# One level of Strassen's scheme in the first product of layer 2, over pairs of feature tiles and 768-token superblocks

## The chip, the cores and the metric

The kernel runs on one core of a Trainium2 chip, in one launch. The metric is the device time of the execution in microseconds (us). Three executions of the kernel before took 1248.97, 1250.37 and 1250.49 us (median 1250.37). One execution was profiled; all durations below come from it.

## The reference

A chunked attention with eight memory keys per head feeds two feed-forward layers of 3072 tokens, 512 model and 2048 hidden features. All is computed to float32 accuracy.

```python
# attention: per chunk of 32 queries, keys from 16 before to 8 after, plus 8 memory keys
x = attn_out.transpose(0, 2, 1, 3).reshape(B * S, H * D)      # 3072 x 512
h = x @ w_in;  sp = log1p(exp(h));  x = (h * tanh(sp)) @ w_out            # layer 1
h = x @ w2_in; g = h * (1 / (1 + exp(-1.702 * h))); out = g @ w2_out      # layer 2
```

## The kernel before, in words

Tokens are cut into 8 blocks of 384 (`TB`), hidden features into 16 tiles of 128 (`NF`), model features into 4 tiles of 128 (`KD`). Every float32 operand of a product is split into two fp32r parts, a high one and the rest (`xh`, `xl`; `wi` and `wo` hold both parts side by side; `gh`, `gl`), and a product is three matmuls: high by high, low by high, high by low.

A step of layer 1 or 2 is one block j and one feature tile f. Its first product (`gemm1`, L792) has 4 x 3 matmuls of 384 columns that fill one PSUM bank `h` (there are two). In layer 2 ScalarE then computes a tanh (L806), VectorE multiplies by h (L808), rounds to `gh` (L815) and subtracts to get `gl` (L821). The second product (`gemm2`, L840) adds into banks `o`: in layer 2 three token tiles, 3 matmuls of 512 columns each. After 16 steps the three banks are evacuated (L858 on ScalarE or L861 on VectorE) into the buffers `e` and `ev`, two of each, and written out.

Layer 1 works while attention for the next block runs beside it. Its result goes to DRAM (`x1d`) and is fetched for layer 2 through staging tiles `st` (a ring of two buffers). The weights arrive as 64-bit words and are converted to float32; those of layer 2 are converted during layer 1, kept in DRAM (`w2d`), and fetched and split once near the end of layer 1 (`w2_fetch`), after which they stay in SBUF.

The order on every engine is set by a planner in the kernel (class `Plan`): each operation has a rank and a guessed duration per engine, an operation goes to an engine when its inputs are ready and its rank is lowest, and the resulting order is then written out, fixed. The guesses are formulas such as `dve(n) = (65 + 1.052 n) / 1000` us for a VectorE operation of n columns. On the chip each engine works through its list in that order, and a wait of the first instruction holds all behind it. All loads and stores around the change are issued by SyncE's queue (SP), in order too.

Of the kernel before, what the change touches and what calls it, by code (L numbers as in the profile page):

```python
# [238 lines left out]
def kernel(  # L239
# [29 lines left out]
    L1 = NB * NF  # L269
    NQ = H // 2 * (GB // 2)  # L270
# [507 lines left out]
    xin = {}  # L778
    outs = {}

    def step(layer, j, f):
        i = ((layer - 1) * NB + j) * NF + f
        xh, xl = x0[j] if layer == 1 else xin[j]
        wh, wl = wi[layer, f]
# [15 lines left out]
        if layer == 1:  # L800

            add(i + 0.3, [("act", act(TB, True), lambda: nc.scalar.activation(  # L802
                out=u.get(), in_=h.get(), func=AF.Mish))], reads=[h], writes=[u], table="mish")
        else:

            add(i + 0.3, [("act", act(TB, True), lambda: nc.scalar.activation(  # L806
                out=u.get(), in_=h.get(), func=AF.Tanh, scale=0.851))], reads=[h], writes=[u], table="exp")
            add(i + 0.6, [("dve", dve(TB), lambda: stt(  # L808
                out=u.get(), in0=u.get(), scalar=1.0, in1=h.get(), op0=ALU.add, op1=ALU.mult
            ))], reads=[h], updates=[u])  # L810
        gh, gl = (T[n].new([P, TB], F32R) for n in ("gh", "gl"))
        add(
            i + 0.65,
# [7 lines left out]
        add(i + 0.7, [("dve", dve(TB), lambda: nc.vector.tensor_tensor(  # L821
            out=gl.get(), in0=u.get(), in1=gh.get(), op=ALU.subtract))], reads=[u, gh], writes=[gl])

        vh, vl = wo[layer, f]
        first, last = f == 0, f == NF - 1
        width = TB if layer == 1 else DM
        if first:
            outs[layer, j] = [
                (T[f"o{m}"].new([P, width], F32), []) for m in range(KD if layer == 1 else TB // P)
            ]  # L830
        for m, (o, order) in enumerate(outs[layer, j]):
            c = slice(m * P, (m + 1) * P)

            def gemm2(o=o, c=c):
                if layer == 1:
                    prods = ((vh[:, c], gh.get()), (vl[:, c], gh.get()), (vh[:, c], gl.get()))
                else:
                    prods = ((gh[:, c], vh.get()), (gh[:, c], vl.get()), (gl[:, c], vh.get()))
                for n, (a, b) in enumerate(prods):
                    nc.tensor.matmul(  # L840
                        out=o.get(), lhsT=a, rhs=b, start=(first and n == 0), stop=(last and n == 2)
                    )

            add(
                i + 2.3, [("pe", 3 * (width / 2400 + 0.003), gemm2)],
                reads=[vh, vl, gh, gl], writes=[o], chain=order,
            )

    def finish(layer, j):
        rank = ((layer - 1) * NB + j + 1) * NF + 1.4  # L850
        c = 1.0 if layer == 1 else 0.5
        width = TB if layer == 1 else DM
        x1s[j] = fixed()
        for m, (o, order) in enumerate(outs.pop((layer, j))):
            t = T["ev" if layer == 1 or m % 2 else "e"].new([P, width], F32)

            def by_act(o=o, t=t):
                nc.scalar.activation(out=t.get(), in_=o.get(), func=AF.Copy, scale=c)  # L858

            def by_dve(o=o, t=t):  # L860
                nc.vector.tensor_scalar(out=t.get(), in0=o.get(), scalar1=c, scalar2=None, op0=ALU.mult)  # L861

            ways = [("act", act(width, True), by_act), ("dve", dve(width), by_dve)]
            add(rank, ways if m % 2 == 0 else ways[::-1], reads=[o], writes=[t])
            if layer == 1:
                load(rank, x1s[j], [lambda t=t, m=m: (x1d[:, m, j * TB:(j + 1) * TB], t.get())],
                     P * TB * 4, 1536, [t])
            else:
                r0 = j * TB + m * P
                load(rank, x1s[j], [lambda t=t, r0=r0: (out[r0:r0 + P, :], t.get())], P * DM * 4, 2048, [t])  # L870
# [55 lines left out]
    for f in range(NF):  # L926
        w2_fetch(f, L1 - NF + f + 3)
    for j in range(NB):
        if j:
            x1_fetch(j)  # L930
        for f in range(NF):
            step(2, j, f)
# [33 lines left out]
```

## Time and profile before

| | us |
|---|---|
| median of three executions | 1250.37 |
| the profiled execution | 1246.88 |
| its span, first to last instruction | 1245.1 |
| TensorE busy | 1212.2 |
| VectorE busy | 724.9 |
| ScalarE busy | 484.9 |

In the profile a line is one group of instructions with the same code line, engine and operation; PE is TensorE, PEld its weight loads, DVE is VectorE, ACT is ScalarE, SP is the queue that issues DMAs. Matmuls overlap one another in the records, so that a matmul's own time (340 ns) is longer than its share of a full stretch; what one costs is read from the time between the starts of groups.

### The profile page before, as it was taken

To read this page: it belongs to the slowest core of one execution; us is meant where nothing else is said; L and a number is where in the kernel's file an instruction comes from. 1 tells how busy PE (TensorE), PEld (TensorE's weight loads), DVE (VectorE), ACT (ScalarE), POOL (GpSimd) and SP (SyncE) were. 2 spreads that over 40 slices of the span, in tenths; PEclk is the share of its full clock that TensorE was granted. 3 is DMA by queue.
4 is the path that set the end of the run, shared out by engine and by line. 5 is a ranking of instruction groups with operands and counts; after the bars stand their busy time and mean duration, and the time that the engine had idled before them with its cause. 6 is when DMAs were issued, how large, how long until landed. Compare 5 with 4: busy or idle time off the path is not lost.

```text
span 1245.1 us, 18734 instructions
## 1 busy us (share of the span) xinstructions
PE 1212.2 (97%) x6912; PEld 1126.8 (91%) x6912; DVE 724.9 (58%) x2074; ACT 484.9 (39%) x1091; POOL 8.2 (1%) x24
## 2 busy tenths in 40 slices
PE   7788899999999999999999999999999999999998
PEld 6687799999999999999999989999999999999997
DVE  6999976767777767677645534343433434343333
ACT  5777665555555555555434411111111111111111
POOL 1000000000000000000000000000000000000000
PEclk9899999999999999999999999999999999999999
DMA  9952343433333334343134401010010101000000
GB/s 214 256 176 107 79 116 74 115 88 92 97 90 99 97 86 106 81 95 90 52 120 134 148 13 44 9 26 26 1 52 1 51 1 51 1 26 1 26 1 26
DMA packets 167450, 92.36 MB, mean 74 GB/s; under 512 B 129272, under 2 KB 153863, under 8 KB 167359
## 3 DMA queue, kind: packets, MB, share of 16 engines
q1 hardware_dynamic: 167007, 90.42, 27.0%
q0 software_dynamic: 352, 0.75, 0.3%
q8 instruction: 54, 0.88, 0.3%
q14 instruction: 37, 0.30, 0.1%
HBM read 70.17 MB, written 20.97 MB: 73 GB/s over the span
## 4 chain that ended last, share of the span: by engine, by line
PE 90%; DVE 4%; SPq 2%; DMA 2%; ACT 1%; issue 1%; DVEq 0%; ACTq 0%
PE h L792 42%; PE o L840 41%; PE s L704 3%; SPq L297 2%; PE s L604 2%; PE s L678 1%; DMA vt<-in_v_dram 1%; DMA wi<-in_moe_w_in_dram 1%; DVE st L353 1%; DVE st L357 0%; DMA wi<-in_q_dram 0%; DVE wi L381 0%; DVE wo L381 0%; DMA vt<-in_mem_v_dram 0%; DVE gl L821 0%
## 5 line engine op out<-in xcount | busy, mean ns | idle before, releaser
L792 PE MATMUL h<-xh,wi 128*128 128x384 f32 x2048 | 534.4, 342 | 8.7 <-DVE wi L376 3.4
L792 PEld LDWEIGHTS h<-xh,wi 128*128 128x128 f32 x2048 | 373.3, 190 | 29.4 <-DVE wi L381 4.7
L792 PE MATMUL h<-xl,wi 128*128 128x384 f32 x1024 | 346.8, 339 | 0.0
L840 PE MATMUL o<-gh,wo 128*128 128x384 f32 x1024 | 274.9, 350 | 0.0
L840 PE MATMUL o<-wo,gh 128*128 128x512 f32 x768 | 240.1, 394 | 0.0
L808 DVE SCALAR_TENSOR_TENSOR u<-u,h 128x384 f32<-128x384 f32 x128 | 71.0, 555 | 288.9 <-ACT u L806 288.1
L806 ACT ACTIVATE u<-h 128x384 f32<-128x384 f32 x128 | 62.9, 492 | 437.1 <-PE h L792 437.1
L792 PEld LDWEIGHTS h<-xl,wi 128*128 128x128 f32 x1024 | 194.1, 190 | 0.0
L840 PEld LDWEIGHTS o<-gh,wo 128*128 128x128 f32 x1024 | 181.9, 189 | 1.3 <-issue 0.3
L840 PE MATMUL o<-gl,wo 128*128 128x384 f32 x512 | 172.7, 337 | 0.0
L840 PEld LDWEIGHTS o<-wo,gh 128*128 128x128 f32 x768 | 142.7, 188 | 23.2
L821 DVE TENSOR_TENSOR gl<-u,gh 128x384 fp32r<-128x384 f32 x256 | 142.4, 557 | 17.8 <-PE o L840 0.5
L840 PE MATMUL o<-wo,gl 128*128 128x512 f32 x384 | 151.9, 396 | 0.0
L802 ACT ACTIVATE u<-h 128x384 f32<-128x384 f32 x128 | 62.8, 491 | 135.2 <-PE h L792 119.1
L632 ACT ACTIVATE e<-e,mx 96x128 f32<-96x128 f32 x240 | 94.4, 395 | 51.0 <-DVE mx L617 50.8
L815 DVE CAST gh<-u 128x384 fp32r<-128x384 f32 x232 | 83.2, 359 | 36.6 <-ACT u L802 22.8
L840 PEld LDWEIGHTS o<-gl,wo 128*128 128x128 f32 x512 | 96.5, 189 | 0.0
L840 PEld LDWEIGHTS o<-wo,gl 128*128 128x128 f32 x384 | 72.1, 188 | 16.6
L617 DVE CUSTOM_DVE_ANT_0 e<-s,mask 96x128 f32<-96x128 f32 x240 | 56.0, 283 | 41.9 <-PE s L604 40.6
L802 ACT ACT_TABLE_LOAD x55 | 70.6, 1283 | 10.2 <-PE h L792 8.7
L632 ACT ACT_TABLE_LOAD x54 | 69.3, 1283 | 3.4 <-DVE mx L617 2.5
L685 DVE COPY aT<-s 128x384 f32<-128x384 f32 x49 | 27.3, 557 | 43.1 <-PE s L678 42.0
(104 smaller groups left out, 861.2 us busy)
## 6 DMA issues: line engine op xcount, KB each, us to landing
wi<-in_moe_w_in_dram SPq DMA_DIRECT2D x16, 512.0 KB
wo<-in_moe_w_out_dram SPq DMA_DIRECT2D x16, 512.0 KB
st<-in_moe_w_in_dram SPq DMA_DIRECT2D x16, 512.0 KB
st<-in_moe_w_out_dram SPq DMA_DIRECT2D x16, 512.0 KB
w2d<-v SPq DMA_DIRECT2D x32, 256.0 KB
st<-w2d SPq DMA_DIRECT2D x16, 512.0 KB
x1d<-ev SPq DMA_DIRECT2D x32, 192.0 KB
st<-x1d SPq DMA_DIRECT2D x16, 384.0 KB
```

The source lines that it names most:

```text
L297: queue.dma_start(out=o, in_=i)
L617: nc.vector.tensor_tensor_reduce(out=e[:, i, hh, :], in0=s[hh][:, i, :], in1=mask[:GQ, mask_of(g0 + i), :], scale=-scale, scalar=-NEG, op0 ...
L632: nc.scalar.activation(out=e[:, i, hh, :], in_=e[:, i, hh, :], func=AF.Exp, scale=-1.0, bias=mx[:, i, hh:hh + 1], accum_out=sm[:, i, hh:hh ...
L685: ("dve", dve(TB), lambda: nc.vector.tensor_copy(out=aT.get(), in_=t.get())),
L704: nc.tensor.matmul(out=o[:, i].rearrange("p h t -> p (h t)"), lhsT=vt[:, g + i, h:h + 2].rearrange("p h d -> p (h d)"), rhs=aT[:, i].rearr ...
L792: nc.tensor.matmul(out=h.get(), lhsT=a[:, c], rhs=b[:, kk, :], start=(n == 0), stop=(n == 3 * KD - 1))
L802: add(i + 0.3, [("act", act(TB, True), lambda: nc.scalar.activation(out=u.get(), in_=h.get(), func=AF.Mish))], reads=[h], writes=[u], tabl ...
L806: add(i + 0.3, [("act", act(TB, True), lambda: nc.scalar.activation(out=u.get(), in_=h.get(), func=AF.Tanh, scale=0.851))], reads=[h], wri ...
L808: add(i + 0.6, [("dve", dve(TB), lambda: stt(out=u.get(), in0=u.get(), scalar=1.0, in1=h.get(), op0=ALU.add, op1=ALU.mult))], reads=[h], u ...
L815: ("dve", dve(TB, True), lambda: nc.vector.tensor_copy(out=gh.get(), in_=u.get())),
L821: add(i + 0.7, [("dve", dve(TB), lambda: nc.vector.tensor_tensor(out=gl.get(), in0=u.get(), in1=gh.get(), op=ALU.subtract))], reads=[u, gh ...
L840: nc.tensor.matmul(out=o.get(), lhsT=a, rhs=b, start=(first and n == 0), stop=(last and n == 2))
```

## The change

Layer 1 is left as it was. In layer 2 two blocks of 384 tokens form a superblock (4 of them), and the feature tiles f and f + 8 form a pair (8 pairs; 32 pairs in all). The model features are cut into two halves of 256. So the first product of a pair is a 2 x 2 product of blocks (feature tile by half of the model features, times half of the model features by token block), and it is done with seven block products in place of eight, by Winograd's form of Strassen's scheme. Each block product is 2 x 3 matmuls of 384 columns.

The seven left operands are sums and differences of the weights' four blocks (`w2_pair`: four combinations of 256 columns, then high and low parts). In superblock 0 they are computed for each pair in turn from `w2d`, used, and stored to DRAM (`w2c`, `w2o`); superblocks 1 to 3 load them again from there, pair by pair. The seven right operands are combinations of the two token blocks (`x_prep`: per superblock four pieces of 192 columns; per piece two or three subtractions, and for each of its operands a high and a low part). They lie in twelve places, the buffers of `xh`, `xl` and of the first halves of `wi` and `wo`; operands 0 to 4 and 5 to 6 of the next superblock are made at different times.

In `step2` products 0 and 1 fill the two `h` banks, are read (`copy`, `plus`), and products 2 and 3 add to the same banks; the same follows with 4, 5 and 6. Five VectorE additions (`plus`, L1109) and two copies (L1103, ScalarE) per pair form the four blocks of h; each then goes through the same tanh, multiply, round and subtract as before (`gate`). The second products (`second`, L1065; 4 x 3 x 3 matmuls of 512 columns per pair) are those of the pair before, and stand between the first products. They add into six banks (`o0` to `o3`, `s0`, `s1`), which are evacuated into `ev` alone (two buffers).

```diff
+    w2c = dram.tile([NP, 4, P, 2 * DM], F32, name="w2c")
+    w2o = dram.tile([NF, P, 2 * DM], F32, name="w2o")
+    AT = ((0, 0), (1, 1), (0, 1), (2, 0), (1, 0), (3, 0), (2, 1))
...
+    def keep_split(rank, both, n, src, view):
...
+                ("act", act(n), lambda: nc.scalar.activation(out=hi.get(), in_=view(), func=AF.Copy)),
+                ("dve", dve(n, True), lambda: nc.vector.tensor_copy(out=hi.get(), in_=view())),
...
+        add(rank + 0.02, [("dve", dve(n), lambda: nc.vector.tensor_tensor(
+            out=lo.get(), in0=view(), in1=hi.get(), op=ALU.subtract))], reads=[*src, hi], writes=[lo])
...
+    def w2_pair(q):
+        sblk, p = divmod(q, NP)
+        base = L1 + 4 * q
+        A = [T[f"wi{NF // 2 + 4 * (p % 2) + i}"].new([P, 2 * DM], F32R) for i in range(4)]
+        O = [T[f"wo{NF // 2 + 2 * (p % 4) + i}"].new([P, 2 * DM], F32R) for i in range(2)]
+        if sblk:
...
+                    load(base - 3.5 + 0.1 * i, A[i], [lambda i=i: (A[i].get().bitcast(F32), w2c[p, i])],
+                         P * 8 * DM, 4096, [w2cs[p, i]])
...
+            return
...
+            st = T["st"].new([P, 2 * DM], F32)
+            load(base - 6 + 0.1 * i, st, [lambda st=st, f=f: (st.get(), w2d[f])], P * 8 * DM, 4096, [w2s[f]])
...
+        deps = [keep_split(base, A[0], DM, [a], lambda: a[:, 0:DM])]
+        s1 = comb(base + 0.1, 0, a21, a22, ALU.add, [b])
+        s2 = comb(base + 0.2, 1, lambda: x[:, 0], a11, ALU.subtract, [a, s1])
+        deps.append(keep_split(base + 0.4, A[1], DM, [s1, s2], lambda: x[:, 0:2].rearrange("p a c -> p (a c)")))
+        s3 = comb(base + 1.0, 2, a11, a21, ALU.subtract, [a, b])
+        s4 = comb(base + 1.1, 3, a12, lambda: x[:, 1], ALU.subtract, [a, s2])
...
+                load(base + 3, w2cs[p, i], [lambda i=i: (w2c[p, i], A[i].get().bitcast(F32))], P * 8 * DM, 4096, deps[i])
...
+    places = ["xh", "xl", "wi0", "wi2", "wi4", "wo0", "wo2", "xh", "xl", "wi6", "wo4", "wo6"]
...
+    def x_prep(sblk, wanted, pieces, rank, gap=0.0):
...
+            st = T["st"].new([P, 2, 2, HALF], F32)
...
+                t1 = comb(rank, 2, lambda st=st, w=w: sub(
+                    out=w[:, 0:2], in0=st[:, :, 1], in1=st[:, 0], op=ALU.subtract), [st])
...
+                add(rank + 0.15, [("dve", dve(HALF), lambda hi=hi, lo=lo, view=view: sub(
+                    out=lo(), in0=view(), in1=hi(), op=ALU.subtract))], reads=[dep, part], writes=[bufs[-1]])
...
+    def product(q, n, rank, bank, fresh):
...
+                for a, b in ((wh, xh), (wl, xh), (wh, xl)):
+                    nc.tensor.matmul(
+                        out=bank.get(), lhsT=a, rhs=b, start=(fresh and m == 0), stop=(m == 3 * K2 - 1),
+                        skip_group_check=not fresh,
+                    )
...
+    def second(q, n, rank):
...
+                t = T["ev"].new([P, DM], F32)
+                evacuate(rank + 0.3, o, t, 0.5, m % 2 == 0)
...
+    def step2(q):
+        r = L1 + 4 * q
+        ha, hb = (T["h"].new([P, TB], F32) for _ in range(2))
+        product(q, 0, r, ha, True)
+        p1 = T["v"].new([P, TB], F32)
+        copy(r + 0.05, p1, ha)
+        product(q, 1, r + 0.2, hb, True)
+        u2 = T["e"].new([P, TB], F32)
+        plus(r + 0.25, u2, p1, hb)
+        if q:
+            second(q - 1, 0, r + 0.5)
+        product(q, 2, r + 1, ha, False)
+        gate(q, 0, r + 1.05, View(ha))
+        product(q, 3, r + 1.2, hb, False)
+        u3 = T["e"].new([P, TB], F32)
+        plus(r + 1.25, u3, p1, hb)
...
+        hc, hd = (T["h"].new([P, TB], F32) for _ in range(2))
+        product(q, 4, r + 2, hc, True)
+        p5 = T["v"].new([P, TB], F32)
+        copy(r + 2.05, p5, hc)
+        product(q, 5, r + 2.2, hd, True)
+        plus(r + 2.22, p5, p5, u3)
+        plus(r + 2.25, u3, u3, hd)
+        gate(q, 2, r + 2.3, View(u3))
...
+        product(q, 6, r + 3, hc, False)
+        plus(r + 3.05, u2, u2, hc)
+        gate(q, 1, r + 3.1, View(u2))
+        gate(q, 3, r + 3.2, View(p5))
...
-    x1_fetch(0)
-    for f in range(NF):
-        w2_fetch(f, L1 - NF + f + 3)
...
+    x_prep(0, range(7), range(4), L1 - NF + 3, 1.5)
...
+        if 2 <= qn % NP < 6 and qn + NP < NQ2:
+            x_prep(qn // NP + 1, range(5), [qn % NP - 2], L1 + 4 * qn + 6)
+        if qn % NP == NP - 1 and qn + 1 < NQ2:
+            x_prep(qn // NP + 1, range(5, 7), range(4), L1 + 4 * qn + 1.5, 0.7)
```

The lists of TensorE, VectorE, ScalarE and SP are those of before until about 13 steps before the end of layer 1; from there they differ. First TensorE in layer 2, before, where feature tile 14 of the last block is followed by the second product of tile 12 (`h` the bank of the first product, `o0` to `o2` those of the second):

```order
L792 MATMUL h_10740<-xh_9815,wi14_7868 128x384 x2
L792 MATMUL h_10740<-xl_9822,wi14_7868 128x384
L840 MATMUL o0_10402<-wo12_7826,gh_10707 128x512 x2
L840 MATMUL o0_10402<-wo12_7826,gl_10709 128x512
L840 MATMUL o1_10408<-wo12_7826,gh_10707 128x512 x2
L840 MATMUL o1_10408<-wo12_7826,gl_10709 128x512
```

And TensorE in pair 6 of superblock 0, after the change: products 0 and 1 fill banks `h_8900` and `h_8914`, a second product of pair 5 follows, and then products 2 and 3 add to the same two banks (the operands of the first products lie in `xh`, `xl`, `wi0` to `wi3` here).

```order
L1038 MATMUL h_8900<-xh_7209,wi8_8622 128x384 x6
L1038 MATMUL h_8914<-xl_7211,wi9_8668 128x384 x6
L1065 MATMUL o0_8020<-wo10_8418,aT_8804 128x512 x2
L1065 MATMUL o0_8020<-wo10_8418,aT_8810 128x512
L1065 MATMUL o1_8030<-wo10_8418,aT_8804 128x512 x2
L1065 MATMUL o1_8030<-wo10_8418,aT_8810 128x512
L1065 MATMUL o2_8071<-wo10_8418,aT_8804 128x512 x2
L1065 MATMUL o2_8071<-wo10_8418,aT_8810 128x512
L1038 MATMUL h_8900<-wi0_7254,wi8_8622 128x384 x2
L1038 MATMUL h_8900<-wi1_7293,wi8_8622 128x384
L1038 MATMUL h_8914<-wi2_7338,wi10_8714 128x384 x2
L1038 MATMUL h_8914<-wi3_7384,wi10_8714 128x384
```

The last matmuls before and behind a second product now write the same bank, and a read of the bank by ScalarE or VectorE has to lie between them.

VectorE in superblock 0, after the change, from the multiply of pair 4's first gate to its next addition that frees a bank of the pair (`h_8659`); `wo13`, `wi8`, `wi9` take parts of the operands of later pairs, `st` and `vt` are staging and combination tiles:

```order
L1088 SCALAR_TENSOR_TENSOR u_8620<-u_8620,h_8562 128x384
L1109 TENSOR_TENSOR e_8632<-v_8588,h_8577 128x384
L421 TENSOR_TENSOR wi8_8622<-st_8520,wi8_8622 128x512
L925 TENSOR_TENSOR kl_8640<-u_8620,ql_8634 128x384
L462 TENSOR_TENSOR vt_8624<-vt_8624,st_8520 128x256
L462 TENSOR_TENSOR vt_8624<-st_8520,st_8595 128x256
L462 TENSOR_TENSOR vt_8624<-st_8520,vt_8624 128x256
L421 TENSOR_TENSOR wo13_8626<-st_8595,wo13_8626 128x512
L417 CAST wi9_8668<-vt_8624 128x512
L1109 TENSOR_TENSOR v_8666<-v_8666,e_8632 128x384
L421 TENSOR_TENSOR wi9_8668<-vt_8624,wi9_8668 128x512
L1109 TENSOR_TENSOR e_8632<-e_8632,h_8659 128x384
```

Between two additions that TensorE waits for there are now up to eight VectorE operations on weights; before, VectorE had four operations per step of layer 2 and none of these.

## Rows read from the trace of the kernel before

**Rows 1.** The page: busy time per engine, and VectorE's busy tenths in 40 slices.

```profile
PE 1212.2 (97%) x6912; PEld 1126.8 (91%) x6912; DVE 724.9 (58%) x2074; ACT 484.9 (39%) x1091; POOL 8.2 (1%) x24
...
DVE  6999976767777767677645534343433434343333
```

**Rows 2.** Stretches: length, busy us (instructions) per engine, granted clock, DMA share, GB/s.

```profile
0.00:150.00 150.00, 121.26 (x783) 107.06 (x784) 132.38 (x422) 107.60 (x273) 6.20 (x15) 0.94 0.65 167
150.00:640.00 490.00, 490.00 (x3069) 470.12 (x3068) 350.37 (x1182) 265.23 (x606) 1.99 (x9) 1.00 0.37 92
711.00:1240.00 529.00, 529.00 (x2653) 478.26 (x2652) 202.09 (x399) 79.08 (x156) 0.00 (x0) 1.00 0.07 22
```

**Rows 3.** Chain of waits that ended last, within layer 2: start, us, what.

```profile
755.49 2.09 PE h L792 x12
757.58 2.08 PE o L840 x9
```

**Rows 4.** Layer 2 groups, 750:1200 us: count, busy us, mean ns, idle before.

```profile
L821 DVE TENSOR_TENSOR gl<-u,gh 128x384 fp32r<-128x384 f32 x108 | 60.2, 557 | 10.3 <-PE o L840 0.5
L808 DVE SCALAR_TENSOR_TENSOR u<-u,h 128x384 f32<-128x384 f32 x108 | 59.9, 554 | 246.4 <-ACT u L806 245.6
L806 ACT ACTIVATE u<-h 128x384 f32<-128x384 f32 x107 | 52.6, 491 | 372.6 <-PE h L792 372.6
L815 DVE CAST gh<-u 128x384 fp32r<-128x384 f32 x102 | 36.8, 361 | 10.5
```

**Rows 5.** Groups of the whole span, other widths.

```profile
L381 DVE TENSOR_TENSOR wo<-st,wo 128x512 fp32r<-128x512 f32 x24 | 16.5, 688 | 15.7 <-ACT wo L375 15.7
...
L886 DVE TENSOR_TENSOR xl<-st,xh 128x768 fp32r<-128x768 f32 x16 | 15.3, 953 | 5.3 <-ACT xh L883 5.2
...
L375 ACT ACTIVATE wo<-st 128x512 fp32r<-128x512 f32 x17 | 10.8, 632 | 22.0 <-PE o L840 21.3 <-DVE st L357 0.7
...
L736 DVE TENSOR_TENSOR xl<-o,xh 128x192 fp32r<-128x192 f32 x8 | 2.8, 344 | 0.0
...
L376 DVE CAST wo<-st 128x512 fp32r<-128x512 f32 x7 | 3.0, 424 | 0.2
```

**Rows 6.** Timeline of the end, last evacuation: start, us, engine, line, operation.

```profile
1241.01 0.60 ACT L858 ACTIVATE e<-o 128x512 f32<-128x512 f32 x1 [0.80 <-PE o L840]
1241.63 0.33 SPq L297 DMA_DIRECT2D out_dram<-e  x1
```

**Rows 7.** Timeline: two loads into staging tiles, and their first readers.

```profile
636.16 0.43 SPq L297 DMA_DIRECT2D st<-x1d  x1
...
640.57 0.85 ACT L883 ACTIVATE xh<-st 128x768 fp32r<-128x768 f32 x1 [3.68 <-DMA st<-x1d]
...
710.91 0.37 SPq L297 DMA_DIRECT2D st<-x1d  x1
...
714.46 0.85 ACT L883 ACTIVATE xh<-st 128x768 fp32r<-128x768 f32 x1 [1.97 <-DMA st<-x1d]
```

**Rows 8.** Timeline: evacuations of one layer 1 block into the two buffers ev.

```profile
563.32 1.08 DVE L861 TENSOR_SCALAR ev<-o 128x384 f32<-128x384 f32 x2
...
563.91 4.31 SPq L297 DMA_DIRECT2D x1d<-ev  x4
...
565.88 0.49 ACT L858 ACTIVATE ev<-o 128x384 f32<-128x384 f32 x1 [1.62 <-DMA x1d<-ev]
```

**Rows 9.** The stretch of the fastest DMA, columns as rows 2.

```profile
60.00:70.00 10.00, 10.00 (x66) 9.75 (x62) 8.95 (x27) 8.45 (x20) 0.00 (x0) 1.00 1.05 370
```

**Rows 10.** Stretches in attention, columns as rows 2.

```profile
100.00:150.00 50.00, 42.71 (x246) 38.53 (x247) 49.09 (x133) 35.69 (x78) 0.21 (x1) 0.97 0.20 49
110.00:115.00 5.00, 3.02 (x13) 2.44 (x12) 4.88 (x13) 4.03 (x9) 0.00 (x0) 0.89 0.00 0
115.00:120.00 5.00, 5.00 (x27) 4.58 (x27) 4.52 (x13) 2.06 (x4) 0.00 (x0) 0.77 0.00 0
```

More of the change, by code (lines that the diff above doesn't have):

```diff
@@ L777, with step @@
     x1s, pace = {}, {}
-    xin = {}
     outs = {}
[L781 to L784, printed above, removed]
+    def step(j, f):
+        i = j * NF + f
+        xh, xl = x0[j]
+        wh, wl = wi[1, f]
         h = T["h"].new([P, TB], F32)
@@ L799, in step, with gemm2, g_split @@
         u = T["u"].new([P, TB], F32)
[L800 to L810, printed above, removed]
-        gh, gl = (T[n].new([P, TB], F32R) for n in ("gh", "gl"))
+        add(i + 0.3, [("act", act(TB, True), lambda: nc.scalar.activation(
+            out=u.get(), in_=h.get(), func=AF.Mish))], reads=[h], writes=[u], table="mish")
+        gh, gl = (T[n].new([P, TB], F32R) for n in ("gh", "gl"))
+        g_split(i + 0.65, u, gh, gl)
+        vh, vl = wo[1, f]
+        first, last = f == 0, f == NF - 1
+        if first:
+            outs[j] = [(T[f"o{m}"].new([P, TB], F32), []) for m in range(KD)]
+        for m, (o, order) in enumerate(outs[j]):
+            c = slice(m * P, (m + 1) * P)
+            def gemm2(o=o, c=c):
+                for n, (a, b) in enumerate(((vh, gh), (vl, gh), (vh, gl))):
+                    nc.tensor.matmul(
+                        out=o.get(), lhsT=a[:, c], rhs=b.get(), start=(first and n == 0), stop=(last and n == 2)
+                    )
+            add(
+                i + 2.3, [("pe", 3 * (TB / 2400 + 0.003), gemm2)],
+                reads=[vh, vl, gh, gl], writes=[o], chain=order,
+            )
+    def g_split(rank, u, gh, gl):
         add(
-            i + 0.65,
+            rank,
             [
@@ L819, in step @@
         )
-        add(i + 0.7, [("dve", dve(TB), lambda: nc.vector.tensor_tensor(
+        add(rank + 0.05, [("dve", dve(TB), lambda: nc.vector.tensor_tensor(
             out=gl.get(), in0=u.get(), in1=gh.get(), op=ALU.subtract))], reads=[u, gh], writes=[gl])
[L824 to L830, printed above, removed]
@@ L831, in step, with evacuate, by_act, by_dve @@
[L831 to L839 removed]
+    def evacuate(rank, o, t, c, act_first):
+        width = t.shape[1]
+        def by_act():
+            nc.scalar.activation(out=t.get(), in_=o.get(), func=AF.Copy, scale=c)
+        def by_dve():
+            nc.vector.tensor_scalar(out=t.get(), in0=o.get(), scalar1=c, scalar2=None, op0=ALU.mult)
+        ways = [("act", act(width, True), by_act), ("dve", dve(width), by_dve)]
+        add(rank, ways if act_first else ways[::-1], reads=[o], writes=[t])
@@ new lines, in finish @@
+    def finish(j):
+        rank = (j + 1) * NF + 1.4
+        x1s[j] = fixed()
+        for m, (o, order) in enumerate(outs.pop(j)):
+            t = T["ev"].new([P, TB], F32)
+            evacuate(rank, o, t, 1.0, m % 2 == 0)
+            load(rank, x1s[j], [lambda t=t, m=m: (x1d[:, m, j * TB:(j + 1) * TB], t.get())], P * TB * 4, 1536, [t])
+    HALF = TB // 2
+    K2 = KD // 2
+    ring = [0]
+    places = ["xh", "xl", "wi0", "wi2", "wi4", "wo0", "wo2", "xh", "xl", "wi6", "wo4", "wo6"]
+    xs = {}
@@ new lines, in second, with go @@
+    def second(q, n, rank):
+        sblk, p = divmod(q, NP)
+        i, th = divmod(n, 2)
+        first, last = p == 0 and i == 0, p == NP - 1 and i == 1
+        w, deps = wo[2, q, i]
+        gh, gl = gs.pop((q, n))
+        if p == 0 and i == 0:
+            names = ("o0", "o1", "o2") if th == 0 else ("o3", "s0", "s1")
+            order2[sblk, th] = [(T[nm].new([P, DM], F32), []) for nm in names]
+        for m, (o, order) in enumerate(order2[sblk, th]):
+            c = slice(m * P, (m + 1) * P)
+            def go(o=o, c=c):
+                for k, (a, b) in enumerate(((gh, 0), (gh, DM), (gl, 0))):
@@ L840, in gemm2 @@
                     nc.tensor.matmul(
-                        out=o.get(), lhsT=a, rhs=b, start=(first and n == 0), stop=(last and n == 2)
+                        out=o.get(), lhsT=a[:, c], rhs=w[:, b:b + DM], start=(first and k == 0), stop=(last and k == 2)
                     )
[L844 to L870, printed above, removed]
```

209 lines of the change are left out of this document (180 added, 29 removed).

## The prediction

> **What bounds the kernel now.** I read the page first: TensorE is busy 97% of the span, VectorE 58%, and VectorE's busy tenths fall from 7 to 4 and 3 in the last third [rows 1]. Then the stretches [rows 2]: from 150 us on TensorE has no idle time at all, and in layer 2 (711 us to the end) VectorE works 202 of 529 us and ScalarE 79. So layer 2 is bound by TensorE alone; whatever leaves its list there comes off the end, and VectorE has 327 us free. The chain of waits says the same: in layer 2 it is an unbroken alternation of the two products [rows 3], 12 matmuls of 384 columns in 2.09 us and 9 of 512 columns in 2.08 us. That gives 0.174 us for one of 384 and 0.232 us for one of 512; these, and not the 340 ns that a matmul shows by itself, are the prices.
>
> **TensorE, removed.** A step of layer 2 is 2.09 + 2.08 = 4.17 us, 128 steps 534 us, which is what layer 2 takes. After the change a pair over 768 tokens has 7 x 6 = 42 matmuls of 384 in place of 48, and 36 of 512 as before; the list has 1344 of the first in layer 2 where there were 1536. So 192 x 0.174 = 33.4 us go. A pair costs 42 x 0.174 + 36 x 0.232 = 15.66 us, 32 of them 501 us. All of it is on the path.
>
> **VectorE and ScalarE, added in every pair.** Per pair VectorE has four gates of 0.554 + 0.361 + 0.557 us and five additions of 384 columns. An addition has no row of its own; the multiply reads the same kinds of operands (one in PSUM) in 0.554 us and the subtraction of two SBUF tiles takes 0.557 [rows 4], so it is between these. Sum: 5.89 + 2.78 = 8.67 us in 15.66. ScalarE has four tanh and two copies at 0.49 [rows 4]: 2.9 us. Both fit, if each wait closes in time. Take the tightest: product 6 ends, the addition that empties its bank starts some 0.2 us later and takes 0.56, and product 0 of the next pair, which overwrites the bank, starts after a second product of 9 x 0.232 = 2.09 us. Slack 1.3 us. The next: first gates 2 and 3 finish behind it (0.56 + 0.56 + 2 x 0.36 + 2 x 0.56 = 2.9 us), then comes the addition that frees a bank for product 3, which starts 3.1 us after product 1 ends; it is done 0.8 us after product 1 and has 2.3 us left. So in a pair with nothing but this, TensorE does not wait, and I cost the additions at 0 in the 22 pairs where the list has nothing else or little. If this cover were gone by 0.1 us a pair, it would cost 2 us.
>
> **Superblock 0, where VectorE also makes the weights.** Widths that have no row lie on the line through 192, 384, 512 and 768 columns (0.344, 0.557, 0.688, 0.953 us [rows 4, 5]): 256 columns take 0.42 us, two-source operations of 192 take 0.35. A pair's weights need four combinations of 256 (1.7 us), five low parts of 512 (3.4), one of 256 (0.4) and one or two roundings of 512 that the planner leaves on VectorE (0.4 each [rows 5]); a piece of the next superblock's tokens needs 0.56 + 0.35 + 5 x 0.35 = 2.7 us. Counted along the list from the first gate of one pair to that of the next, VectorE has 10.7, 17.1, 15.7, 16.0, 16.2 and 15.2 us in pairs 0 to 5, although the planner moved the gates' roundings to ScalarE there (which with weights at 0.63 us a rounding [rows 5] comes to 7.5 to 9.6 us a pair and fits); TensorE has 15.66. The planner believed in (65 + 1.052 x 384) / 1000 = 0.469 us where the row has 0.557, so it saw 14 us of work and room for it. Walked along the list in pair 4, from the addition that frees product 6's bank to the same one a pair later: 16.2 us of work, some 8 places where an operation needs the result in front of it (up to 0.1 us each, 0.5 together). TensorE's first matmul of product 0 waits at the end of this round, and its whole list stands behind it. One round then takes 16.7 to 17.1 us, 1.0 to 1.4 more than TensorE's. Four such pairs and 0.3 in pair 5, less the 1.3 us of slack at the start: 3 to 5 us. To this come the staging tiles, of which there are two: between the last read of one and the first read of the tile that takes its place the list has 3.7 to 4.5 us of VectorE work, twice a pair, while a load took 3.55 us from issue to its reader with little beside it and 4.41 with a second load in flight [rows 7], and a token piece now has two issues (0.37 us more). That is 0 to 1.2 us of wait at two tiles a pair; I take 0.9 a pair. Together 8.5 us. Bounds: 2 (only the excess of the sums) and 15 (3 us in each of pairs 1 to 5).
>
> **The superblock boundaries.** When a superblock ends, five places become free at once and the planner puts token pieces into the list at once: 19.1 us of VectorE work in pairs 7 and 15, 14.5 in pairs 8 and 16, so 33.6 in 31.3 us of TensorE's. Worse is where they stand: twelve operations (5.0 us with the gate) lie in front of the multiply that frees product 2's bank for product 4, and 4.5 us of such in front of the next addition. Walked the same way, product 4 of pair 8 starts 1.8 us late and product 0 of pair 9 3.2 us late in all; with the places of dependence (0.5 a pair) and some wait for tiles I take 4.8 us, twice: 9.6. Bounds 2 and 16. At the third boundary only two token pieces remain (12.2 us), which I cost at 0: the free 3.5 us of that pair hide them.
>
> **The end.** Before, three banks go to `e`, `ev`, `e` and none waits; the last evacuation starts 0.2 us after the last matmul, and 4.1 us later the span ends [rows 6]. Now six tiles go through the two buffers `ev`. A buffer is free 2.0 us after its tile is written [rows 8] (192 KB; 256 KB may take 0.2 more). Three tiles in a row per buffer, 0.6 + 2.2 us each, the first ready 3.3 us before TensorE's end: the third starts at about 3.1 us after it in place of 0.2, so 2.9 us more. Bounds 0 and 5.
>
> **The start.** In the last 13 steps of layer 1 VectorE gets the seven operands of superblock 0 (4 x 3.7 us) and the weights of pairs 0 to 2, some 30 us over 54 us in which layer 1 asks 0.92 us a step. It fits; pair 0 has no second products to cover its waits, for which I take 1 us (0 to 4).
>
> **Transfers.** Superblocks 1 to 3 load 2.9 MB a pair, 184 GB/s, a pair ahead; superblock 0 moves 4.3 MB a pair, 276 GB/s. The best stretch moved 370 [rows 9]. I cost the streaming itself at 0.
>
> **Sum.** -33.4 + 8.5 + 9.6 + 2.9 + 1.0 = -11.4 us. The profiled execution took 1246.9 (span 1245.1, 1.8 around it), so 1235.5 of that kind; it lies 3.5 under the median of 1250.4. On the median's scale: 1239.
>
> **Rivals.**
> A. VectorE's backlog is absorbed. For it: the sums exceed TensorE's by little, and before, VectorE was busy 132 of 150 us in attention [rows 2] without gaps of its own. Against: the list's order cannot change. Then only the excess less the slack counts, 1.1 us in superblock 0 and at each of two boundaries, and the end: 6.2 us, so 1250.4 - 27.2 = 1223.
> B. Slower: the two staging tiles decide. Place: the first VectorE row on each new tile, 15 in pairs 1 to 5 and 8 at each of two boundaries, 31 in all, each with the whole VectorE list behind it and TensorE behind that. Each store of 0.5 MB in front of a load costs 0.5 / 370 = 1.4 us, and one or two stand there in superblock 0. Each 0.1 us more than I walked costs 3.1 us; from 0.45 us on (13.9 us) the kernel is slower than before. At 0.6 us more it takes 1239 + 18.6 = 1258. Against it: half the tiles have over 5 us of work to cover them. The Trainium skill, "DMA: Bandwidth & Descriptors", section "Latency and other measured facts", says that an HBM access grows from 0.2 us to 2 us at high load; the trace agrees in kind (3.55 and 4.41 us), and by the page's 1.8 us at all 31 tiles it would be an estimated 1295.
> C. TensorE's pauses cost its clock. In attention, where it idled 7.3 of 50 us, the granted clock was 0.97, and after an idle of 2 us in 110 to 115 us it was 0.77 in the next 5 us [rows 10], that is 46% of them at 1.2 GHz. My pairs with waits last some 158 us; 0.03 of that is 4.7 us: 1244. Against: my waits are 1 us or less each. The Trainium skill, "TensorE: Matmul & The Clock Gate", section "A second HAM failure mode: psum-queue depth-cycling", says that a kernel cycling through PSUM banks with short idles between groups of matmuls makes the clock swing; in layer 1 and 2 the same two banks were cycled at 1.00 [rows 2], so the trace does not show it without idle time.
> D. The waits cost twice what I walked, (8.5 + 9.6) more: 1257; half as much again, 1248, is no change.
> That the change does not remove what it says is excluded by the count of matmuls.
>
> **How the numbers follow.** Forecast 0.52, A 0.20, B 0.12, C 0.07, D 0.09. A measurement can tell about 0.2% (2.5 us) from no change. Faster: forecast, A, C, 0.79; D lies half in the same and half slower, and the forecast's upper end reaches the same: same 0.08, slower 0.13. All terms at their lower bounds give 1250.4 - 29.4 = 1221, at their upper 1250.4 + 6.6 = 1257. I give 1222 to 1254, which leaves out the far part of B and D.
>
> **What would show it.** In layer 2 a plain pair (10 to 14) of 15.7 us with no idle TensorE; 1344 matmuls on the line of the first products; pairs 1 to 5 at 16.5 to 18 us each with VectorE busy over 90% and TensorE waiting for VectorE's additions (L1109, L1088); pairs 7 to 9 and 15 to 17 together some 5 us longer than three plain ones; the last ScalarE evacuation 3 us after the last matmul. Idle before the first reader of `st`, put down to a DMA and over 1 us a tile, would speak for B; TensorE idle in plain pairs would make the sum wrong at its root.

## The result, and the profile after

The changed kernel took 1218.80 us (median of 4 runs, 1216.50 to 1222.72) where the kernel before took 1249.67 (4 runs): a ratio of 0.9757, 95% interval 0.9727 to 0.9786. The forecast was 1239, with a range from 1222 to 1254. It had the direction right, and the kernel is faster than its range allowed. The profiled execution took 1217.31 us, with a span of 1215.5; before, 1246.88 and 1245.1.

Two lines of the page after, busy time per engine and VectorE's busy tenths, answer to [rows 1]:

```profile
PE 1181.2 (97%) x6720; PEld 1092.9 (90%) x6720; DVE 846.1 (70%) x2445; ACT 547.6 (45%) x1272; POOL 8.2 (1%) x24
...
DVE  6899977676767777767655688878556855565553
```

192 matmuls are gone. The VectorE tenths of the last part rose from 4 and 3 to 5 to 8, and never reach 9 there. The stretches answer to [rows 2] (length, busy us and instructions of PE, PEld, DVE, ACT, POOL, granted clock, DMA share, GB/s):

```profile
150.00:640.00 490.00, 490.00 (x3068) 469.84 (x3067) 351.78 (x1189) 264.64 (x607) 2.00 (x9) 1.00 0.36 92
711.00:1208.00 497.00, 495.87 (x2453) 442.82 (x2453) 316.33 (x723) 148.34 (x338) 0.00 (x0) 1.00 0.63 212
```

Layer 1 is what it was. In layer 2 VectorE is busy half as much again and ScalarE almost twice as much (before, VectorE had three operations a step, 399 in some 126 steps, and not the four of the description above), the DMA engines move some nine times as much, and TensorE still idles for only 1.1 of 497 us, at full clock. So there is no place here for the 18 us of waits that the forecast had in superblock 0 and at two boundaries.

The first 150 us differ from run to run (attention, untouched by the change). To keep them out I count from one event in layer 1 that both kernels have, the evacuation that stands at 565.88 before [rows 8] and here after:

```profile
564.55 0.49 ACT L932 ACTIVATE ev<-o 128x384 f32<-128x384 f32 x1 [1.65 <-DMA x1d<-ev]
```

From there to the end of the span are 679.2 us before and 651.0 after: 28.3 less. This is the difference that the terms of the forecast have to make up; the other 1.3 us between the two spans lie in the first 565 us.

Now the pairs of superblock 0 one by one. Stretches of the kernel after, cut at the starts of product 0 (pairs 2, 4, 5, then 9, then 11, which has nothing but its own work):

```profile
727.64:743.28 15.64, 15.64 (x80) 14.11 (x78) 12.96 (x32) 7.59 (x19) 0.00 (x0) 1.00 0.76 266
...
758.99:774.73 15.74, 15.74 (x79) 14.10 (x78) 13.98 (x33) 8.52 (x20) 0.00 (x0) 1.00 0.73 262
774.73:791.03 16.30, 15.90 (x80) 13.97 (x78) 13.67 (x34) 7.11 (x15) 0.00 (x0) 1.00 0.76 266
...
838.17:854.38 16.21, 15.91 (x79) 13.99 (x78) 10.37 (x24) 4.86 (x10) 0.00 (x0) 1.00 0.78 266
...
870.13:885.85 15.72, 15.72 (x79) 14.09 (x78) 8.11 (x18) 2.94 (x6) 0.00 (x0) 1.00 0.55 183
```

A plain pair takes 15.72 us (forecast 15.66). Pair 4, for which the forecast walked 16.2 us of VectorE work and a round of 16.7 to 17.1, takes 15.74, and VectorE is busy for 13.98 of them. By the groups of this stretch, its 33 instructions, count times mean duration, add up to 16.76 us, no less than the forecast had counted for its round. So the work was there, and it took less time than its rows add up to. How both can be seen in the timeline of VectorE in pair 4 (start, us, engine, line, operation):

```profile
759.27 0.35 DVE L995 TENSOR_TENSOR vt<-st,vt 128x192 f32<-128x192 f32 x1
759.53 0.69 DVE L421 TENSOR_TENSOR wi<-vt,wi 128x512 fp32r<-128x512 f32 x1
760.14 0.55 DVE L1088 SCALAR_TENSOR_TENSOR u<-u,e 128x384 f32<-128x384 f32 x1
760.61 0.55 DVE L1088 SCALAR_TENSOR_TENSOR u<-u,v 128x384 f32<-128x384 f32 x1
761.08 0.35 DVE L1016 TENSOR_TENSOR xl<-vt,xl 128x192 fp32r<-128x192 f32 x1
761.34 0.55 DVE L925 TENSOR_TENSOR aT<-u,aT 128x384 fp32r<-128x384 f32 x1
761.81 0.55 DVE L925 TENSOR_TENSOR kT<-u,qT 128x384 fp32r<-128x384 f32 x1
```

The multiply at 760.14 lasts 0.55 us, and the next one starts 0.47 us behind its start. The 512 columns at 759.53 last 0.69 and hold the engine for 0.61; the 192 at 759.27 last 0.35 and hold it for 0.26. So the next operation, when it needs nothing of the one in front, starts some 0.08 us before the end of that one's row. The trace of before has it too, in layer 1, on VectorE's timeline:

```profile
649.31 0.56 DVE L821 TENSOR_TENSOR gl<-u,gh 128x384 fp32r<-128x384 f32 x1
649.79 0.69 DVE L381 TENSOR_TENSOR wo<-st,wo 128x512 fp32r<-128x512 f32 x1
```

All that TensorE waited in layer 2, by the list of its waits (total us, times, longest):

```profile
PE h L1038 <- DVE e L1109: 0.4, 1, 0.4
PE h L1038 <- ACT v L1103: 0.4, 1, 0.4
PE h L1038 <- DVE u L1088: 0.3, 1, 0.3
```

By the distance of the starts, less the price of the matmuls in between, they cost 0.59, 0.57 and 0.47 us, 1.6 in all, one each in pairs 1, 5 and 9. Only the first lies behind a queue of VectorE operations. The second is a staging tile's: ScalarE's rounding waits for it, and the copy that frees the bank stands behind the rounding (ScalarE's timeline):

```profile
778.40 0.63 ACT L416 ACTIVATE wo<-st 128x512 fp32r<-128x512 f32 x1 [1.05 <-DMA st<-w2d]
778.93 0.47 ACT L1103 ACTIVATE v<-h 128x384 f32<-128x384 f32 x1
```

The third stands at product 4 of pair 9, the product at which the forecast had 1.8 us in pair 8. Its cause is another. VectorE's multiply is early and waits 3.52 us for ScalarE's tanh, which stands behind an evacuation that waits for a free buffer of `ev` (timeline of both engines):

```profile
845.37 0.60 ACT L932 ACTIVATE ev<-s 128x512 f32<-128x512 f32 x1 [4.49 <-DMA out_dram<-ev]
845.86 0.49 ACT L1086 ACTIVATE u<-h 128x384 f32<-128x384 f32 x1
...
846.38 0.56 DVE L1088 SCALAR_TENSOR_TENSOR u<-u,h 128x384 f32<-128x384 f32 x1 [3.52 <-ACT u L1086]
```

This list leaves out waits that end before the modelled end of the matmul in front. Pair 17, which stands to the second boundary as pair 9 does to the first, has no row in it and still takes 16.31 us, 0.6 more than a plain pair: at three places the distance between two starts is 0.30 to 0.32 us in place of 0.17 or 0.23, and 0.28 at the next. Each place lies behind an operation of VectorE, and in front of the first and the last of these ScalarE had waited for a buffer of `ev` again (the stretch, and ScalarE's timeline):

```profile
964.31:980.62 16.31, 16.31 (x79) 13.94 (x78) 11.20 (x26) 4.86 (x10) 0.00 (x0) 1.00 0.83 268
```

```profile
962.40 0.60 ACT L932 ACTIVATE ev<-o 128x512 f32<-128x512 f32 x1 [2.53 <-DMA out_dram<-ev]
...
971.58 0.60 ACT L932 ACTIVATE ev<-s 128x512 f32<-128x512 f32 x1 [3.73 <-DMA out_dram<-ev]
```

The end of the span answers to [rows 6] (timelines of TensorE, VectorE and ScalarE):

```profile
1208.57 0.40 PE L1065 MATMUL s<-wo,gl 128*128 128x512 f32 x1
...
1211.17 0.69 DVE L935 TENSOR_SCALAR ev<-s 128x512 f32<-128x512 f32 x1 [4.28 <-DMA out_dram<-ev]
...
1211.86 0.60 ACT L932 ACTIVATE ev<-s 128x512 f32<-128x512 f32 x1 [2.16 <-DMA out_dram<-ev]
```

The last two evacuations wait for the two buffers `ev`. From the end of the last matmul (1208.97) to the end of the span are 6.5 us, before 4.2: 2.4 us more (forecast 2.9).

The account from the common event on: 33.4 us of matmuls less; 1.6 of listed waits, 0.6 in pair 17 and 2.4 of the end more; that gives 28.8, against 28.3 measured. The other 0.5 us, 0.015 in each of 32 pairs, have no cause shown.

### The profile page after: what moved, and what is told of

It reads as the page before. It is cut to its first block, busy times and chain, and to the rows that moved or that the text cites. A ratio compares the mean times of both kernels' runs of the same rounds, so it can differ in the third digit from the quotient of the medians.

```text
span 1215.5 us, 19240 instructions
## 1 busy us (share of the span) xinstructions
PE 1181.2 (97%) x6720; PEld 1092.9 (90%) x6720; DVE 846.1 (70%) x2445; ACT 547.6 (45%) x1272; POOL 8.2 (1%) x24
## 4 chain that ended last, share of the span: by engine, by line
PE 83%; DVE 7%; DMA 6%; SPq 3%; issue 1%; ACT 1%; ACTq 0%; DVEq 0%
PE h L883 21%; PE o L906 20%; PE h L1038 16%; PE o L1065 12%; PE s L1065 6%; PE s L796 3%; SPq L299 3%; PE s L696 2%; PE s L770 1%; DMA out_dram<-ev 1%; DMA st<-w2d 1%; DMA st<-x1d 1%; DVE st L355 1%; DMA vt<-in_v_dram 1%; DMA wi<-in_moe_w_in_dram 1%
## 5 line engine op out<-in xcount | busy, mean ns | idle before, releaser
L883 PE MATMUL h<-xh,wi 128*128 128x384 f32 x1024 | 271.7, 345 | 8.1 <-DVE wi L378 3.4
L883 PEld LDWEIGHTS h<-xh,wi 128*128 128x128 f32 x1024 | 184.8, 190 | 17.8 <-DVE wi L383 4.7
L883 PE MATMUL h<-xl,wi 128*128 128x384 f32 x512 | 173.7, 339 | 0.0
L892 ACT ACTIVATE u<-h 128x384 f32<-128x384 f32 x128 | 62.8, 490 | 143.7 <-PE h L883 133.5
L883 PEld LDWEIGHTS h<-xl,wi 128*128 128x128 f32 x512 | 97.4, 190 | 0.0
L1038 PE MATMUL h<-wi,wi 128*128 128x384 f32 x480 | 94.9, 337 | 0.8 <-DVE e L1109 0.4
L1038 PEld LDWEIGHTS h<-wi,wi 128*128 128x128 f32 x480 | 85.3, 188 | 6.7 <-DVE e L1109 1.2
L1103 ACT ACTIVATE v<-h 128x384 f32<-128x384 f32 x64 | 31.3, 489 | 118.2 <-PE h L1038 118.2
L1065 PE MATMUL o<-wo,gh 128*128 128x512 f32 x262 | 82.0, 394 | 0.0
L1038 PE MATMUL h<-wo,wi 128*128 128x384 f32 x384 | 77.7, 338 | 0.3 <-DVE u L1088 0.3
L1086 ACT ACTIVATE u<-e 128x384 f32<-128x384 f32 x64 | 33.4, 524 | 98.5 <-DVE e L1109 98.1
L1038 PEld LDWEIGHTS h<-wo,wi 128*128 128x128 f32 x384 | 68.1, 188 | 3.9 <-DVE u L1088 1.1
```

The source lines that it names most:

```text
L883: nc.tensor.matmul(out=h.get(), lhsT=a[:, c], rhs=b[:, kk, :], start=(n == 0), stop=(n == 3 * KD - 1))
L1038: nc.tensor.matmul(out=bank.get(), lhsT=a, rhs=b, start=(fresh and m == 0), stop=(m == 3 * K2 - 1), skip_group_check=not fresh,)
L1065: nc.tensor.matmul(out=o.get(), lhsT=a[:, c], rhs=w[:, b:b + DM], start=(first and k == 0), stop=(last and k == 2))
L1086: add(rank, [("act", act(TB, True), lambda: nc.scalar.activation(out=u.get(), in_=src(), func=AF.Tanh, scale=0.851))], reads=[src.buf], wr ...
```

## The experiments

Two theories were to be told apart. S: what a VectorE operation costs its list is the distance between starts, so VectorE had room in every pair. R: it costs the length of its row, and something else absorbed the excess. In the diffs a line that starts with + or - is the edit to the changed kernel. Medians, ratios to the kernel before in the same series with their intervals, and the time from the common event to the end of the span in the profiled execution:

| | median us | ratio | from the event, us |
|---|---|---|---|
| before (beside the first run of the changed kernel; beside e1 to e5; beside e6 to e9) | 1249.67; 1248.67; 1246.10 | | 679.2 |
| changed | 1218.80 | 0.9757 [0.9727, 0.9786] | 651.0 |
| changed, again (e6) | 1218.94 | 0.9789 [0.9768, 0.9809] | 650.3 |
| three buffers (e2) | 1218.73 | 0.9763 [0.9740, 0.9785] | 647.6 |
| three buffers, again (e7) | 1219.22 | 0.9786 [0.9760, 0.9812] | 647.7 |
| eight products (e5) | 1251.18 | 1.0019 [1.0004, 1.0034] | 681.7 |
| ten more (e4) | 1238.58 | 0.9914 [0.9890, 0.9937] | 671.7 |
| three more (e8) | 1225.22 | 0.9825 [0.9808, 0.9842] | 655.5 |
| late tiles (e9) | 1236.21 | 0.9918 [0.9894, 0.9942] | 667.8 |

**VectorE alone.** Behind the end of the kernel, 96 additions that need nothing of each other and 24 that do (one run):

```
...
+        for n in (384, 192, 256, 512):
+            for i in range(24):
+                d = dst[1 + i % 12]
+                k = (i // 12) * DM
+                nc.vector.tensor_tensor(out=d[:, k:k + n], in0=src[0][:, :n], in1=src[1][:, :n], op=ALU.add)
+        for i in range(24):
+            nc.vector.tensor_tensor(out=dst[0][:, :TB], in0=dst[0][:, :TB], in1=src[1][:, :TB], op=ALU.add)
```

> The changed kernel with a tail on VectorE alone: 24 additions each of 384, 192, 256 and 512 columns that read the same two SBUF tiles and write different places, then 24 of 384 columns in place, each needing the one before. Theory S (an operation occupies VectorE for the distance between two starts, which is shorter than its row; the row's end overlaps the next operation when that one is independent): starts 0.47, 0.27, 0.33 and 0.60 us apart, rows of 0.55, 0.35, 0.42 and 0.69; in the dependent chain 0.62 to 0.66 apart. Theory R (the row is what an operation costs, as the prediction reckoned): 0.55, 0.35, 0.42, 0.69 apart, and the same 0.55 to 0.66 in the chain.

The groups of that stretch (count, busy us, mean ns of one, idle before):

```profile
L1211 DVE TENSOR_TENSOR wi<-st 128x512 f32<-128x512 f32 x24 | 14.5, 685 | 0.0
L1213 DVE TENSOR_TENSOR wi<-wi,st 128x384 f32<-128x384 f32 x24 | 13.4, 557 | 0.8
L1211 DVE TENSOR_TENSOR wi<-st 128x384 f32<-128x384 f32 x24 | 11.3, 549 | 0.0
L1211 DVE TENSOR_TENSOR wi<-st 128x256 f32<-128x256 f32 x24 | 8.1, 419 | 0.0
L1211 DVE TENSOR_TENSOR wi<-st 128x192 f32<-128x192 f32 x24 | 6.5, 352 | 0.0
```

Busy time counts overlapping rows once, so busy by count is the distance of starts: 0.47, 0.27, 0.34 and 0.60 us at 384, 192, 256 and 512 columns, where the rows are 0.549, 0.352, 0.419 and 0.685 long. The dependent chain took 14.16 us, 0.59 each, for the same 384 columns; here S had expected 0.62 to 0.66 and missed. For independent operations S holds and R falls; the price of a dependence is 0.12 us over the distance of starts. The distances are those of the planner's formula, which the forecast had set aside for the row. The Trainium skill, "VectorE: DVE Perf Modes", section "The DRAIN you can't avoid", says that the next operation does not start until the pipe is empty, and adds that one which is not held starts earlier; here the second half is what decides, by 0.08 us an operation.

**Eight products.** Product 0 is computed twice in every pair, so TensorE has its 192 matmuls back and all else is as changed:

```
+            for _ in range(2 if n == 0 else 1):
+                once()
...
```

> The changed kernel, but product 0 of every pair is computed twice into the same bank (six more matmuls of 384 columns a pair, 192 in all), so that TensorE has as many matmuls as before, and everything else of the change stays. If the whole gain is TensorE's 192 matmuls: 33.4 us more, less the 1.6 us of waits that this covers, 1250 to 1252, that is the kernel before and the 2.4 us of the longer end. Rival: part of the gain came from elsewhere (the fetches of tokens and weights that were dropped or moved): clearly under 1249.

1251.18 us, 2.5 more than before. Its stretch in layer 2, columns as above:

```profile
725.00:1240.00 515.00, 515.00 (x2583) 465.54 (x2582) 310.58 (x710) 142.57 (x325) 0.00 (x0) 1.00 0.59 199
```

TensorE never waits. The remaining 2.5 us (681.7 against 679.2 from the event) are the longer end, 6.6 us behind the last matmul in place of 4.2. So the combinations, the streaming and the new order cost nothing as long as TensorE has its 16.7 us a pair (48 x 0.174 + 36 x 0.232), and the whole gain is the matmuls.

**Ten more and three more.** Each low part of a pair's weights and each combination is computed a second time into a tile that nobody reads (ten more VectorE operations a pair in superblock 0), or only three low parts of 512 columns:

```
+                nc.vector.tensor_tensor(out=idle[:, :n], in0=view(), in1=hi.get(), op=ALU.subtract)
...
+                nc.vector.tensor_tensor(out=idle[:, :H2], in0=in0(), in1=in1(), op=op)
```

> The changed kernel; in superblock 0 each of the four combinations and six low parts of a pair's weights is followed by the same operation into a scratch tile (ten more VectorE operations a pair, the order of all else as it was). Theory S: 4 x 0.33 + 5 x 0.60 + 0.33 = 4.7 us more a pair on some 13.5 of 15.66, so some 2.5 to 3 us over in each of five pairs: 11 to 18 us more than the changed kernel, and TensorE waiting for L1109 and L1088 there. Theory R: 4 x 0.42 + 5 x 0.69 + 0.42 = 5.5 us on a list already full: 27 us more. If VectorE did not matter at all: 0.

> Each pair of weights has three more VectorE subtractions of 512 columns, whose result is not used; 15 of them fall into pairs 1 to 5 of superblock 0, 9 before. Theory S (VectorE is occupied for the distance between starts, 0.60 us at 512 columns, and 13.0 to 14.0 of a pair's 15.7 us are taken): 1.8 us more a pair go into some 2 us that are free, so 0 to 6 us more than the changed kernel. Theory R (occupied for the length of the row, 0.688 us, and no time free): 5 x 2.06 = 10 us more, or 14 with what the gates wait.

Ten more cost 19.8 us by the medians (of two series) and 20.7 to 21.4 from the event: above what S said, below R, nearer S. Cut at the starts of product 0, 13.9 us of it lie in pairs 1 to 5, the five that S counted, 2.6 in pair 0 and 3.4 in pair 6. VectorE is now the bound in superblock 0 (two stretches of 17 us, VectorE only: busy, instructions, clock, DMA share, GB/s):

```profile
718.00:735.00 17.00, 17.00 (x39) 1.00 0.72 252
735.00:752.00 17.00, 15.81 (x37) 1.00 0.58 218
```

A part of the cost in pair 6 is TensorE's clock: an idle of 1.6 us ended at 812.0, and the 5 us behind it had 17 matmuls at a granted clock of 0.68. Behind an idle of 2.1 us, which ended at 745.0, it stayed at 1.00 (all engines):

```profile
812.00:817.00 5.00, 5.00 (x17) 4.51 (x18) 4.97 (x13) 1.32 (x3) 0.00 (x0) 0.68 0.99 291
745.04:750.04 5.00, 5.00 (x26) 4.63 (x27) 4.97 (x11) 1.41 (x3) 0.00 (x0) 1.00 0.45 159
```

Three more cost 6.3 us by the medians of one series (1225.22 against 1218.94) and 4.5 to 5.2 from the event. That is the upper end of S and some half of R's lower value. Pairs 1 to 5 got 15 x 0.60 = 9 us more work and grew by 3.4 us together, the whole kernel by 4.5 to 6.3; so some 3 to 5.6 us were absorbed. The room was there, but it was smaller than the 1.7 to 2.7 us a pair that S read from busy time. Part of that idle time was waits for staging tiles, of weights (`w2d`) and of tokens (`x1d`): between 640 and 815 us 9.4 us in the changed kernel (rows below, under late tiles) and 11.3 in its second profile. With three more they fell to 7.6 and did not go, by the list of VectorE's waits (total us, times, longest):

```profile
DVE vt L467 <- DMA st<-w2d: 6.4, 6, 1.6
...
DVE vt L995 <- DMA st<-x1d: 1.2, 1, 1.2
```

So the added work took the place of some of these waits and not of most. That a tile's wait hangs on when its buffer comes free, which more work delays too, would explain it; no run shows this by itself.

**Late tiles.** In front of each load of a weight tile into `st` a copy of 0.5 MB within DRAM:

```
+                nc.sync.dma_start(out=w2j[f], in_=w2d[f])
+                return st.get(), w2d[f]
...
```

> In front of each load of a weight tile into a staging tile (16 in superblock 0, 10 of them beside layer 2) the queue issues a copy of 0.5 MB within DRAM, which nobody reads; so each of these loads lands 1.4 us later (0.5 MB at 370 GB/s) or up to twice that, since the copy reads and writes. Rival B of the forecast (the tiles decide, each wait has VectorE's and TensorE's lists behind it): 10 x 1.4 = 14 us more than the changed kernel, up to 28. Theory S (VectorE has about 2 us free in each pair and already waits for tiles in them unseen): 0 to 5 us more, while the waits of VectorE's first operations on the tiles, 10.9 us together in the changed kernel, at least double.

17.3 us by the medians, 16.8 to 17.5 from the event: rival B's price, and S was wrong in this one. VectorE's waits for tiles between 640 and 815 us, in the changed kernel and here (total us, times, longest); with 1.1 us at a third place they rise from 9.4 to 21.3, which S had expected too, at no such price:

```profile
DVE vt L462 <- DMA st<-w2d: 6.8, 5, 2.1
...
DVE vt L990 <- DMA st<-x1d: 2.6, 3, 1.2
```

```profile
DVE vt L467 <- DMA st<-w2d: 16.6, 6, 5.2
...
DVE vt L995 <- DMA st<-x1d: 3.6, 4, 1.5
```

From issue to first reader the eight weight tiles that are read in pairs 2 to 5 took 0.3 to 3.3 us longer than in the changed kernel, 1.6 in the mean. This is the one with the longest delay, by the queue's and VectorE's timelines; it had its reader 7.9 us after its issue, where the changed kernel's tile for the same operation at 733.58 took 4.6:

```profile
740.02 0.32 SPq L299 DMA_DIRECT2D st<-w2d  x1
...
747.94 0.76 DVE L467 TENSOR_TENSOR vt<-st 128x256 f32<-128x256 f32 x2 [4.16 <-DMA st<-w2d]
```

And the stretches of that wait and of the time behind it, all engines:

```profile
746.00:749.80 3.80, 1.06 (x5) 0.53 (x3) 1.86 (x6) 1.01 (x2) 0.00 (x0) 1.00 0.34 138
749.80:755.00 5.20, 5.11 (x18) 4.68 (x19) 4.81 (x11) 1.70 (x4) 0.00 (x0) 0.67 0.64 218
```

TensorE idled 2.8 us, and in the 5.2 us behind that the granted clock was 0.67 and 18 matmuls were done. This happened three times (behind idles of 2.7, 2.8 and 2.0 us); behind a first idle of 2.8 us, at 712 us, the clock stayed at 1.00. From the distances of the starts, waits make up 11 of the 17 us (12.3 less the 1.2 that the changed kernel has in the same stretch), and slow matmuls 4.8. So the mechanism of B is real, and the staging tiles are close to being a limit: in the changed kernel tiles made VectorE wait up to 2.1 us, inside the time that S's prices leave free, and these few us later they no longer fitted.

**Three buffers for the end, twice.** The six last tiles go through `ev`, `e` and `v`:

```
-                t = T["ev"].new([P, DM], F32)
+                name = "ev"
+                if sblk == NS - 1:
+                    name = ("ev", "e", "v")[m]
+                t = T[name].new([P, DM], F32)
```

> The changed kernel, with the six output tiles of the last superblock in two buffers each of ev, e and v in place of six through the two of ev. If the last tiles wait for the transfers of those before, the end behind the last matmul shrinks from 6.7 us to some 4.3 as in the kernel before: 2.4 us less (1.5 to 3), about 1216.4. Rival: the transfers at the end follow one another on the queues anyway: no change.

> The six tiles of the last superblock leave through ev, e and v instead of ev alone, timed on the chip on which the changed kernel is timed too. Theory E (the end is a wait for the two buffers ev): 2.4 to 2.9 us less than the changed kernel of the same job, which is what its end cost against before (last matmul to the end of the span 6.7 us in place of 4.3). Theory N (the wait lies beside the write of the last tile, which ends the run anyway): within 0.5 us of it.

> The changed kernel once more, as the neighbour of the other three runs of this job. Every theory: 1218 us, within the 1216.5 to 1222.7 of its first runs, 0.9757 of the kernel before.

The first profile, timelines of VectorE, TensorE and ScalarE at the end:

```profile
1208.94 0.69 DVE L935 TENSOR_SCALAR e<-s 128x512 f32<-128x512 f32 x1 [1.41 <-PE s L1065]
...
1209.21 0.40 PE L1065 MATMUL s<-wo,gl 128*128 128x512 f32 x1
...
1209.65 0.60 ACT L932 ACTIVATE v<-s 128x512 f32<-128x512 f32 x1 [0.81 <-DVE e L935]
```

No evacuation waits for a DMA any more, and the span ends 3.7 us behind the last matmul in both profiles of this kernel, 6.5 and 6.6 in both of the changed one: 2.8 us, as theory E said. From the event it is 2.6 to 3.4 us shorter. The medians don't show it (1218.73 and 1219.22 against 1218.80 and 1218.94): single runs of either kernel lie between 1215 and 1224, and in the profiled ones most of that lies in front of the event, in the first 150 us. In the second profile the granted clock of the first 100 us was 0.76, in the first 0.95, and the event came at 574.05 in place of 565.72. So it is the best version by its end, and not shown faster as a whole.

## Why the forecast was wrong

**The step that failed** is the price of VectorE's work in "Superblock 0, where VectorE also makes the weights": "Walked along the list in pair 4, [...] 16.2 us of work, some 8 places where an operation needs the result in front of it (up to 0.1 us each, 0.5 together)". Row durations were added up as if one began where the other ended. The count was right as a sum of rows (16.76 us in the stretch of pair 4 above, which is cut at another place), and the engine was busy for 13.98. The text had the contradiction before it: "The planner believed in (65 + 1.052 x 384) / 1000 = 0.469 us where the row has 0.557, so it saw 14 us of work and room for it." The planner's 14 us were right. What could have told: by the groups of the whole trace of before, count times mean is 810 us for VectorE, and the page has it busy for 724.9 [rows 1], which an engine with rows end to end can't have; and in [rows 8] two evacuations in a row, each 0.557 by the prices used, last 1.08 us together. The 0.1 us for an operation that needs the result in front of it stood in no row; measured alone it is 0.12, over the distance of starts.

What hung on that price:
- Superblock 0: 8.5 us forecast, 1.2 measured (pairs 1 and 5), under its lower bound of 2. Over half of the forecast's 8.5 were waits for tiles (0.9 a pair). These came about, and larger (VectorE waited 6.6 us for tiles in pairs 1 to 5), but in time that VectorE had free; the only loss behind a tile was pair 5's 0.57 us, where ScalarE waited for it. The bounds were both worked out with the same wrong price, so the range did not hold the time.
- The boundaries: 9.6 forecast, 0.5 measured at the first and 0.6 at the second (1.3 there in the first profile with three buffers), under the lower bound of 2. The place was nearly right (at the first boundary product 4, a pair later); what stood in front in the rows above was the ring `ev`, which the forecast charged at the end alone. No run gives the boundaries more buffers, so this cause is read from the trace and not tested.
- The start: 1.0 us for pair 0, of which nothing was seen.

**What held.** 33.4 us of matmuls, shown by the eight products (681.7 - 651.0 = 30.7 us from the event, and with the 2.2 us of waits that the longer list covers 32.9). The additions at no cost in plain pairs (15.72 us against 15.66; no waits). The streaming at no cost: 183 to 189 GB/s in plain pairs (forecast 184), 258 to 309 in pairs 1 to 7 (forecast 276). The end, 2.4 for 2.9. By these alone and the waits seen, the forecast would have been 1250.4 - 33.4 + 1.6 + 0.6 + 2.4, some 1222.

**The rivals.** A, at 1223, was the nearest, but for a reason it did not have: there was no backlog to absorb. B did not decide here, and is the one to fear (late tiles). C had no place, since TensorE never idled for as long as 1 us in layer 2; late tiles and ten more showed that its mechanism exists in this stage. D multiplied waits that were not there. (Of the chances, B and half of D give 0.165 for slower, where the forecast has 0.13; nothing here hangs on it.)

## What to carry to other kernels

Price an engine's list by the distance between starts of neighbours that need nothing of each other, and add the price of a dependence where there is one; a sum of row lengths that exceeds the engine's busy time says that rows overlap. Bounds worked out with one price hold only if the price does, so check a price against a second view (busy time of a full stretch) before building terms on it. Where an engine seems to have room, look for waits inside its idle time first: three more operations a pair filled them only in part.

## What was unexpected of the hardware

- VectorE starts an independent operation 0.08 us before the one in front of it has its end in the trace, at 192 to 512 columns alike; a dependent one of 384 columns costs 0.59 us instead of 0.47. ScalarE's rows overlap too: the copy at 778.93 starts 0.53 us behind the start of a row of 0.63.
- With late tiles, after three of four idles of TensorE of 2.0 to 2.8 us the mean granted clock of the next 5 us was 0.66 or 0.67, that is about two thirds of them at 1.2 GHz and the rest at 2.4. With ten more, an idle of 2.1 us was followed by 1.00 and one of 1.6 us by 0.68, so the length of an idle alone does not tell which. After the idles of 0.3 to 0.4 us in the changed kernel it stayed at 1.00.
- A copy of 0.5 MB within DRAM in front of a load of 0.5 MB lengthened the time from that load's issue to its reader by 0.3 to 3.3 us (eight tiles), 1.6 in the mean; at the best rate seen, 370 GB/s [rows 9], the copy would take an estimated 1.4.
